# Attention products with v in two steps, some row sums over added halves, and u products over 384 columns

## The chip, the cores and the metric

The kernel runs on one NeuronCore of a Trainium2 chip. The metric is the device time of one execution in microseconds; three executions were timed, and one more was profiled.

## The reference, cut to what matters

Four batches of 576 rows go through block-causal attention (8 heads of 64), then a feed-forward layer with a convolution over neighbouring rows, then a second feed-forward layer that mixes rows.

```python
scores = scale * q @ k.T                        # per head, 576 x 576
scores = where(block_i >= block_j, scores, -1e9)  # blocks of 64 rows
attn = exp(scores - max); attn /= attn.sum(-1) + 1e-9
x = concat_heads(attn @ v)                      # 4 x 576 x 512
h = relu(x @ w_in); c = conv3(h); x = (h * sigmoid(c)) @ w_out       # 512 -> 1024 -> 512
h = relu(x @ w2_in); u, v = split(h, 2)         # 512 each
v = (v - mean(v)) / sqrt(var(v) + 1e-6)
out = (u * (w_spatial @ v + b_spatial)) @ w2_out
```

## The kernel before

The heads are taken two at a time: 16 pairs. Every value is split into a high and a low half where the products need it, so most products are three matmuls with one result (high by high, low by high, high by low).

**Steps.** Work on TensorE (PE) is cut into steps, and the string SEQ (line 64) writes out their order by hand, one letter a step. An x or y is one of the five steps of a pair's row maxima: four products of queries and keys, which VectorE (DVE) reduces, and a transposition (line 1005) after which the maxima go by DMA into a row that enters the scores. An s is a score step (lines 1062 to 1074), after which ScalarE (ACT) takes the exponential (line 1083) into the tiles e0 and e1. A v is the product of the exponentials with v (function av, line 1111; matmuls on line 669). An m is a product of the first feed-forward layer (in1, out1; matmuls on line 661), a p one of the second layer. An f is a filling step: two matmuls of 222 columns with no use for their result. A capital letter takes its PSUM buffer from the other ring. The string has 432 letters, 3 of them f.

**Forms on PE.** The x, s and v steps use the array in parts (64 rows, or 64 or 32 columns); the last of the row-maximum products, the transpositions, m and p use the whole array.

**Other engines.** ORDER (line 70) holds the order of every instruction on DVE, ACT, GpSimd (POOL) and the DMA queue of SyncE (SP); BIND says which buffer each step gets; ENG says on which engine an operation with a choice runs. All four are tables written out in the source, and an engine takes its next entry only when that entry's turn has come. Each engine therefore waits in order.

**Row sums.** For the pairs in ONES_PAIRS (0 to 5) the sums of the exponentials are made on PE, with a column of ones over all five chunks of keys (68 matmuls in the av step, sums included). For the other ten pairs add_up (line 1142) adds the chunks up in a tile es on DVE or POOL (lines 1155 and 1156, table ADD), and PE takes one short sum of it (36 matmuls in the step). The normalisation norm_a multiplies in three pieces for the first kind, in one for the second.

**Second layer.** x2 lies in DRAM. For each batch load_x2s brings it whole into one tile (one buffer), load_tails brings the last 64 rows of two batches into another. Steps: vtile (12 matmuls over 512 columns), ustep (12 matmuls over 288 columns; 8 a batch, 32 in all), sstep (mixing over rows, then the product with u on DVE), ostep (the last product). The raw weights of the last stage go through two buffers of the ring wr.

## Time and profile before

| | us |
|---|---|
| median of 3 runs | 578.49 (577.84 to 578.58) |
| the profiled execution's own time | 578.16 |
| its span in the trace | 576.4 |
| PE busy in it | 566.5 (98%) |
| VectorE busy | 420.9 (73%) |
| ScalarE busy | 259.7 (45%) |
| GpSimd busy | 121.7 (21%) |

The span runs from the first to the last instruction of the trace. Rows of the trace have a start and a duration; a matmul's duration holds its way through the array, so the rate at which PE works is read from start to start. A stretch is counted from the span's start.

### The profile page before, as it was taken

How to read it: one execution, taken by the hardware profiler on the slowest of the kernel's cores; microseconds unless marked ns; L12 is line 12 of the kernel's file. 1: busy time of each engine (PE TensorE's matmuls, PEld its weight loads, DVE VectorE, ACT ScalarE, POOL GpSimd, SP SyncE). 2: the span in 40 equal slices, each digit the busy share in tenths (PEclk: the TensorE clock that was granted, in tenths of full speed). 3: DMA queues.
4: the chain of work that ended last, by engine and by line, in shares of the span. 5: the costliest groups of instructions: out<-in, count | busy, mean ns of one | idle time of the engine just before them, and what ended most of it. 6: DMA issues, size and time to landing. Idle time of an engine off the chain costs nothing.

```text
span 576.4 us, 11721 instructions
## 1 busy us (share of the span) xinstructions
PE 566.5 (98%) x4570; PEld 510.2 (89%) x4570; DVE 420.9 (73%) x954; ACT 259.7 (45%) x554; POOL 121.7 (21%) x166
## 2 busy tenths in 40 slices
PE   7999999999999999999999999999999999999997
PEld 5666689798988888899889999999899989999997
DVE  5888889977498889869574788566996446456557
ACT  6657668643576336437262766443351014014101
POOL 4334312130013312401311020333111111012020
PEclk7999999999999999999999999999999999999999
DMA  7677642031404143130214547138203230330002
GB/s 229 208 216 202 223 155 75 30 108 45 125 25 148 46 127 127 28 121 2 65 43 152 190 144 215 43 115 251 97 1 124 72 91 1 124 102 22 33 31 84
DMA packets 43430, 61.13 MB, mean 106 GB/s; under 512 B 8877, under 2 KB 34221, under 8 KB 43374
## 3 DMA queue, kind: packets, MB, share of 16 engines
q1 hardware_dynamic: 43230, 60.37, 33.7%
q8 instruction: 36, 0.59, 0.4%
q14 instruction: 20, 0.16, 0.1%
q10 hardware_dynamic: 144, 0.00, 0.0%
HBM read 45.99 MB, written 14.23 MB: 104 GB/s over the span
## 4 chain that ended last, share of the span: by engine, by line
PE 95%; DVE 2%; ACT 1%; POOL 1%; issue 0%; DVEq 0%; POOLq 0%; ACTq 0%
PE mo L661 57%; PE s L661 14%; PE st L669 10%; PE st L1070 4%; PE st L1062 4%; PE st L943 2%; PE st L1074 2%; PE st L661 1%; DVE mx L948 1%; PE mo L1384 1%; ACT e L1083 1%; DVE y L1669 0%; PE st L1005 0%; POOL x L698 0%; POOL w1i_l L698 0%
## 5 line engine op out<-in xcount | busy, mean ns | idle before, releaser
L661 PE MATMUL mo<-x,w1i_h 128*128 128x290 f32 x504 | 105.7, 299 | 0.0
L661 PE MATMUL mo<-g,w1o_h 128*128 128x288 f32 x464 | 97.7, 297 | 0.0
L661 PEld LDWEIGHTS mo<-x,w1i_h 128*128 128x128 f32 x504 | 82.4, 188 | 2.1 <-ACT g L691 0.5
L661 PEld LDWEIGHTS mo<-g,w1o_h 128*128 128x128 f32 x464 | 76.0, 189 | 2.0 <-issue 1.6
L1241 DVE SCALAR_TENSOR_TENSOR cc<-h,cwt,cc 128x288 f32<-128x288 f32 x128 | 66.3, 532 | 12.0 <-ACT cc L1238 11.1
L661 PE MATMUL mo<-x,w1i_l 128*128 128x290 f32 x252 | 74.8, 297 | 0.0
L661 PE MATMUL mo<-g,w1o_l 128*128 128x288 f32 x232 | 68.5, 295 | 0.0
L1083 ACT ACTIVATE e<-st 128x1024 f32<-128x1024 f32 (+2 forms) x64 | 53.2, 837 | 21.1 <-PE st L1074 20.4
L661 PE MATMUL mo<-x,w2i_h 128*128 128x288 f32 x256 | 51.8, 295 | 0.0
L948 DVE TENSOR_REDUCE mx<-st 128x2 f32<-128x128 f32 (+2 forms) x64 | 42.4, 684 | 8.6 <-PE st L943 8.3
L661 PEld LDWEIGHTS mo<-x,w1i_l 128*128 128x128 f32 x252 | 47.5, 188 | 0.0
L669 PE MATMUL st<-e,v 128*64 128x448 f32 (+4 forms) x384 | 46.7, 392 | 0.1
L669 PEld LDWEIGHTS st<-e,v 128*64 128x64 f32 x384 | 25.0, 137 | 22.9 <-issue 16.8
L661 PEld LDWEIGHTS mo<-g,w1o_l 128*128 128x128 f32 x232 | 43.6, 188 | 0.0
L672 POOL TENSOR_SCALAR g<-ga 128x288 fp32r<-128x288 f32 x40 | 20.1, 513 | 110.8 <-DVE ga L1589 44.0
L661 PEld LDWEIGHTS mo<-x,w2i_h 128*128 128x128 f32 x256 | 41.2, 188 | 0.4 <-ACT u L1563 0.2
L698 POOL TENSOR_TENSOR g<-cc,g 128x288 fp32r<-128x288 f32 x19 | 18.1, 954 | 106.4 <-ACT g L691 74.0
L661 PE MATMUL s<-w2i_h,x 128*128 128x512 f32 x128 | 39.5, 390 | 0.0
L661 PE MATMUL mo<-ws_h,vnh 128*128 128x288 f32 x135 | 39.4, 296 | 0.0
L661 PE MATMUL mo<-x,w2i_l 128*128 128x288 f32 x128 | 37.7, 295 | 0.0
L1074 PE MATMUL st<-mq,mk 64*128 64x320 f32 (+1 forms) x192 | 37.2, 383 | 0.0
L1238 ACT ACTIVATE cc<-h,cwt 128x288 f32<-128x288 f32 x64 | 33.9, 533 | 5.6 <-DVE g L675 2.8
(200 smaller groups left out, 1327.8 us busy)
## 6 DMA issues: line engine op xcount, KB each, us to landing
x2d<-y SPq DMA_DIRECT2D x32, 288.0 KB
x<-x2d SPq DMA_DIRECT2D x16, 576.0 KB
raw<-in_kq_dram SPq DMA_DIRECT2D x15, 576.0 KB
v<-in_vt_dram SPq DMA_DIRECT2D x16, 320.0 KB
rb<-rd SPq DMA_DIRECT2D x32, 144.0 KB
x<-in_w2i_dram SPq DMA_DIRECT2D x8, 512.0 KB
out_dram<-o SPq DMA_DIRECT2D x28, 144.0 KB
w_raw<-in_w1i_dram SPq DMA_DIRECT2D x4, 512.0 KB
```

Of the source, the lines that this page charges most:

```text
L661: nc.tensor.matmul(o, w, x, start=start, stop=stop)
L669: nc.tensor.matmul(o[row:row + m], w, x, start=start, stop=stop)
L672: nc.gpsimd.tensor_scalar(o, i, 1.0, 0.0, ALU.mult, ALU.add)
L698: P=("POOL", t_ptt(n), lambda: nc.gpsimd.tensor_tensor(o, a, b, ALU.subtract), 0, prio, True))
L943: nc.tensor.matmul(st[:, e, o:o + n], qp[r, 128 * c:128 * c + 128], kp[r, 0:n], start=True, stop=True)
L948: return ("DVE", t_dve(2 * i.shape[-1] * (i.shape[2] if len(i.shape) == 4 else 1)), lambda: nc.vector.tensor_reduce(o, i, AX.X, ALU.max), ...
L1062: nc.tensor.matmul(out, keys(RAW[p][:, 0, :], r), RAW[p][r, 1, q0:q0 + nq], start=True, stop=False)
L1070: nc.tensor.matmul(st[:, e, o:o + nq], keys(kx, slice(64 * e, 64 * e + 64)), qx[e], start=j == 0, stop=False)
L1074: nc.tensor.matmul(st[:, e, o:o + nq], keys(mk, r), q[r, q0:q0 + nq], start=False, stop=True)
L1083: yield ("ACT", t_act(2 * n), lambda: nc.scalar.activation(ex[:, :, e0:e0 + n], st[:, :, 0:n], ACTF.Exp, scale=0.125), 0, 0)
L1238: yield ("ACT", t_act(HT, False, 1), lambda: nc.scalar.activation(cc, h[:, o:o + HT], ACTF.Copy, scale=cwt[:, c, 1:2]), 0, P_G)
L1241: yield ("DVE", t_dve(HT, ptr=1), lambda: nc.vector.scalar_tensor_tensor(cc, h[:, o + e:o + e + HT], cwt[:, c, j:j + 1], cc, ALU.mult, ALU ...
```

## The change

Four things are edited, and every table is written anew. (1) ONES_PAIRS loses pairs 3 to 5: their sums now go by add_up, and their av steps have the shorter form. (2) Each av step becomes two steps, one for the key chunks 0, 1 and 4 and one for the chunks 2 and 3 with the sums; the first doesn't need the last exponential, and SEQ has 32 v for 16. (3) ustep takes 384 columns of a pair of batches: three column pieces a pair of batches, 24 steps for 32; x2 comes in tiles of 384 columns with two buffers, the middle one from both batches; the tile of tails is gone, a tile ux holds 192 columns of u, and the product with u on DVE takes two pieces where it crosses the tiles. (4) The ring wr of the last stage has one buffer for two. SEQ, ORDER, BIND and ENG are all new; SEQ has 450 letters, 13 of them f.

```diff
-ONES_PAIRS = 0x3f
+ONES_PAIRS = 0x7
...
 SEQ = (
-    "xxxyxyxsssfsxxssfxyxxvxssssxyxxvxssssxyxxvxssssxyxxvxssssxyxxvsxsfxssyxxvxsmmmmmxxmmxxxmmmmsssmmssvxmxxxmmssxm"
-    "mmmxMmmmxmmmxxvxsmmmxsssssmmmmmmmxmxxvxssmmmmmxvssssssmmmmxxvxssxmmmmxxmxxvssmmxssmxmxmmxxvsxmsssxmxmxxvsmmxsm"
-    "mssmmmxmmmmmmmmmMmmmmmmsvsssmmmmmvmmmmmmmmmmmmmmmmmmmmMmmmmmmmmmmmppmmmmMmmmpppppppppppppppppppppppppppppppppp"
-    "pPppPpPpPPpPppppppPpppppppppppppppppppPPPPPPppPPPppppPppppppppppppppppppPPPPPPppPppppppppPpppPpPpPpPpp"
+    "xxxysxyxsfssxffffxssffxyxxvvfxsfsssxyxxvvxssssxyxxvvxssssxyxxvvsxsssxfyxxvfsfxfsvxyssxxmmmmmvvxsmmxxmxxxmmssss"
+    "svvxmxmxxxmmmssmmmmmMmxmxmmxxvvsmmmmxsmmmxssssmmmxmvvxxmmxssmmxmssvvmmssssmmmmmxxvvxssxmmmmxxxxmmmsvvsssxmmmxx"
+    "xxmvxsvsssmmmmxxmmxxvvxsmmsmmssxmmmmmvvsmmmMmmmmmmsssmmmmmvvmmmmmmmmmmmmmmmmmmmmMmmmmmmmmmmmpppmmmmMmmmppppppp"
+    "pppppppppppppppppppppppPppPpPpPPpPppppppPpppppppppppppppppppPPPPPPppPPPppppPppppppppppppppPPPPPPppPppppppppPpp"
+    "pPpPpPpPpp"
 )
...
-    "K": "AAPPDPAAADDADAADP",
+    "K": "DPAPPAPPDADPDPADD",
-    "ADD": "PPPPPPPPDDDDPPPPDDDDDDDDDDDDDDPDDDDDDDPDDDDDDDPPDDDDDDDPDDDPDDDD",
+    "ADD": "PPPPPPPPDDDDDDDDDPPDDPDDDDDDDDDPPDDDDDDDPDDPDPPPDDDDPPDPDDDDDDDD",
...
-        self.cost = 0.1 if tile != self.tile else 0.0
+        self.cost = 0.15 if tile != self.tile else 0.0
...
-    def av(p):
+    def av(p, part):
+        chunks = ((0, 1, 4), (2, 3))[part]
+
         def fn(got):
-            st = got["st"][0]
-            AVT[p] = st.rearrange("p b n -> p (b n)")
-            a, v = AVT[p], VT[p]
+            if part == 0:
+                AVT[p] = got["st"][0]
+            st = AVT[p]
+            a, v = st.rearrange("p b n -> p (b n)"), VT[p]
             ex = [ES[p, g] for g in range(2)]
             ops = []
-            for c, (k0, q0, et, e0) in enumerate(CH):
+            for c in chunks:
+                k0, q0, et, e0 = CH[c]
                 for lo, hi in ((0, 128), (128, S)) if c == 0 else ((q0, S),):
                     ops += [(a[:, VO + lo:VO + hi], 64 * e, v[:, e, c, :], ex[et][:, e, e0 + lo - q0:e0 + hi - q0],
-                             c == 0, hi == 128 or c == 4) for e in range(2)]
-            if pe_sums(p):
+                             c == 0, hi == 128 or c == 3) for e in range(2)]
+            if part == 1 and pe_sums(p):
                 for c, (k0, q0, et, e0) in enumerate(CH):
                     for lo, hi, o, j in QSEG:
                         lo = max(lo, q0)
                         if lo < hi:
                             ops += [(a[:, lo - o:hi - o], 64 * e + 32 * j, ones4 if c == 4 else ones,
                                      ex[et][:, e, e0 + lo - q0:e0 + hi - q0], c == 0 and lo > 0, c == 4 - j) for e in range(2)]
-            else:
+            elif part == 1:
                 es = SUMS[p]
+                od.cost += 0.18
                 for src, lo, hi, j in ((ex[0], 0, 128, 0), (es, 128, HT, 0), (es, HT, S, 1)):
                     o = 0 if src is ex[0] else 128
                     ops += [(a[:, lo - HT * j:hi - HT * j], 64 * e + 32 * j, ones, src[:, e, lo - o:hi - o], True, True)
                             for e in range(2)]
             tiled(ops)
-            od.cost += 0.18
+            if part == 0:
+                return None
+            AVT[p] = a
             return [(v_out(p, st), "att"), (s_out(p, st), "att"), (st_out(p, st), "att")]
-        return dict(needs=[("e", p, g, i) for g in range(2) for i in range(2)] + [("v", p)] + ([] if pe_sums(p) else [("sum", p)]),
-                    rings=[("st", 1)], fn=fn,
+        if part == 0:
+            return dict(needs=[("e", p, 0, 0), ("e", p, 0, 1), ("e", p, 1, 0), ("v", p)], rings=[("st", 1)], fn=fn, tile=True)
+        return dict(needs=[("e", p, 1, 1)] + ([] if pe_sums(p) else [("sum", p)]), rings=[], fn=fn,
                     frees=lambda: [("v", [VT[p]]), ("e0", [ES[p, 0]]), ("e1", [ES[p, 1]])] + ([] if pe_sums(p) else [("es", [SUMS[p]])]), tile=True)
 
     def add_up(p):
@@ -1296,7 +1306,7 @@
         if p == 0:
             sstream.extend(score(p, 0, i, part) for part in range(2) for i in range(2))
         sstream.extend(score(p, g, i) for g in range(p == 0, 2) for i in range(2))
-        vstream.append(av(p))
+        vstream.extend(av(p, part) for part in range(2))
...
-    X2, XT = {}, {}
+    X2 = {}
+    NT = 384
+    PIECES = [[(0, 0, NT, 0)], [(0, NT, S, 0), (1, 512, S, 192), (1, 0, 128, 256)], [(1, 128, 512, 0)]]
+    U_OUT = [[(0, 0, NT, 0)], [(0, NT, S, 0), (2, 0, 192, 192)], [(1, 128, 512, 0)]]
+    S_IN = [[[(0, 0, HT)], [(0, HT, S)]], [[(2, 64, 192), (1, 128, HT)], [(1, HT, 512), (2, 0, 64)]]]
 
     def load_x2s():
-        for b in range(B):
-            yield ("take", "x20")
-            t = X2[b] = p2w.tile([128, 2, KD, S], F32R, name="x2", tag="x2", bufs=1)
-            for hf in range(2):
-                for m in range(KD):
-                    yield ("wait", ("x2", b, hf, m))
-                od.spawn(load_x2(b, hf, t), "p2")
-
-    def load_x2(b, hf, t):
+        for pr in range(B // 2):
+            for j, pieces in enumerate(PIECES):
+                yield ("take", "x20")
+                t = X2[pr, j] = p2w.tile([128, 2, KD, 384], F32R, name="x2", tag="x2", bufs=2)
+                for e, lo, hi, _ in pieces:
+                    for hf in range(lo >= HT, 1 + (hi > HT)):
+                        for m in range(KD):
+                            yield ("wait", ("x2", 2 * pr + e, hf, m))
+                od.spawn(load_x2(pr, j, t), "p2")
+
+    def load_x2(pr, j, t):
         def ld():
-            for i in range(2):
-                nc.sync.dma_start(out=raw(t[:, i, :, HT * hf:HT * hf + HT]), in_=x2d[b][i, :, :, HT * hf:HT * hf + HT])
-        yield from dma(od, 2 * 589824, ld, 0, 1.35)
-        yield ("mark", ("x2l", b, hf))
-
-    def load_tails():
-        for b in range(0, B, 2):
-            yield ("take", "xt")
-            t = p2w.tile([128, 2, KD, 128], F32R, name="xt", tag="xt", bufs=1)
-            XT[b] = t
-            for e in range(2):
-                for m in range(KD):
-                    yield ("wait", ("x2", b + e, 1, m))
-
-                def ld(b=b, e=e, t=t):
-                    for i in range(2):
-                        nc.sync.dma_start(out=raw(t[:, i, :, 64 * e:64 * e + 64]), in_=x2d[b + e][i, :, :, 512:S])
-                yield from dma(od, 2 * 262144, ld, 0 if b == 0 else 2, 1.35)
-            yield ("mark", ("xt", b))
+            for e, lo, hi, at in PIECES[j]:
+                for i in range(2):
+                    nc.sync.dma_start(out=raw(t[:, i, :, at:at + hi - lo]), in_=x2d[2 * pr + e][i, :, :, lo:hi])
+        yield from dma(od, 2 * 786432, ld, 0, 1.35 if len(PIECES[j]) == 1 else 3.2)
+        yield ("mark", ("x2l", pr, j))
...
+        at, o = ((b // 2, 0 if c < 3 else 1), (0, 128, 256, 0, 128)[c]) if b % 2 == 0 else ((b // 2, 2 if c else 1), (256, 0, 128, 256)[c])
...
-    def ustep(b, hf, m):
+        return dict(needs=[("w2i", 1, k) for k in range(KD)] + [("x2l",) + at], rings=[("st", 1)], fn=fn,
+                    frees=lambda: [("x20", [None])] if b % 2 and c == 0 else [])
+
+    def ustep(pr, j, m):
         def fn(got):
-            x2 = X2[b]
+            x2 = X2[pr, j]
             ring = me["ring"]
             slot = got[ring][0]
             ps = bank(slot)
             i = 0
             for k in range(KD):
                 for w, xi in ((w2i_h, 0), (w2i_l, 0), (w2i_h, 1)):
-                    mm(ps[:, 0:HT], w[:, k, 128 * m:128 * m + 128], x2[:, xi, k, HT * hf:HT * hf + HT],
-                       i == 0, i == 3 * KD - 1)
+                    mm(ps[:, 0:NT], w[:, k, 128 * m:128 * m + 128], x2[:, xi, k, :], i == 0, i == 3 * KD - 1)
                     i += 1
-            if hf == 0 and m == 0:
-                U[b] = p2w.tile([128, KD, S], F32, name="u", tag="u", bufs=1)
-            u = U[b]
+            if m == 0:
+                if j == 1:
+                    U[pr, 2] = P2[0].tile([128, KD, 192], F32, name="ux", tag="ux", bufs=1)
+                else:
+                    U[pr, j // 2] = p2w.tile([128, KD, S], F32, name="u", tag="u", bufs=1)
 
             def task():
-                yield ("ACT", t_act(HT), lambda: nc.scalar.activation(
-                    u[:, m, HT * hf:HT * hf + HT], ps[:, 0:HT], ACTF.Relu), 0, 0)
+                for e, lo, hi, at in U_OUT[j]:
+                    yield ("ACT", t_act(hi - lo), lambda: nc.scalar.activation(
+                        U[pr, e][:, m, lo:hi], ps[:, at:at + hi - lo], ACTF.Relu), 0, 0)
                 yield ("free", ring, slot)
-                yield ("mark", ("u", b, hf, m))
+                yield ("mark", ("u", pr, j, m))
             return [(task(), "p2")]
-        me = dict(needs=[("w2i", 0, k) for k in range(KD)] + [("x2l", b, hf)],
-                    base=[("u", 1)] if hf == 0 and m == 0 else [], fn=fn,
-                    frees=lambda: [("x20", [None])] if (hf, m) == (1, 3) else [])
+        me = dict(needs=[("w2i", 0, k) for k in range(KD)] + [("x2l", pr, j)],
+                    base=[("ux" if j == 1 else "u", 1)] if m == 0 else [], fn=fn,
+                    frees=lambda: [("x20", [None])] if j != 1 and m == 3 else [])
...
-                yield ("DVE", t_dve(HT), lambda: nc.vector.tensor_tensor(
-                    ga, u[:, d, HT * hf:HT * hf + HT], ps[:, 0:HT], ALU.mult), 0, 0)
+                at = 0
+                for e, lo, hi in S_IN[b % 2][hf]:
+                    x, y = slice(at, at + hi - lo), U[b // 2, e][:, d, lo:hi]
+                    yield ("DVE", t_dve(hi - lo), lambda: nc.vector.tensor_tensor(ga[:, x], y, ps[:, x], ALU.mult), 0, 0)
+                    at += hi - lo
...
-        pstream.extend(ustep(b, hf, m) for hf, m in tiles)
+        pstream.extend(ustep(b // 2, j, m) for j in ((2,) if b % 2 else (0, 1)) for m in range(KD))
...
-    od.spawn(load_tails(), "p2")
...
-    slots("wr", p2, 2, [128, 1152], F32, "w_raw")
+    slots("wr", p2, 1, [128, 1024], F32, "w_raw")
```

## Rows read from the trace of the kernel before

**Rows 1.** Page, part 1: busy us (share of the span) xinstructions of each engine.
```profile
PE 566.5 (98%) x4570; PEld 510.2 (89%) x4570; DVE 420.9 (73%) x954; ACT 259.7 (45%) x554; POOL 121.7 (21%) x166
```

**Rows 2.** Page, part 4: chain that ended last, share of the span by engine and line.
```profile
PE 95%; DVE 2%; ACT 1%; POOL 1%; issue 0%; DVEq 0%; POOLq 0%; ACTq 0%
```

**Rows 3.** Stretches: us, busy us (x instructions) by engine, PEclk, DMA share, GB/s.
```profile
10.00:20.00 10.00, 10.00 (x69) 6.97 (x70) 8.05 (x20) 7.82 (x17) 2.53 (x3) 0.76 0.73 236
17.25:67.25 50.00, 48.30 (x575) 33.39 (x571) 41.19 (x100) 31.42 (x49) 17.62 (x18) 1.00 0.66 199
67.25:105.60 38.35, 38.05 (x335) 31.95 (x336) 35.45 (x81) 28.79 (x61) 7.81 (x9) 1.00 0.39 127
304.00:572.00 268.00, 268.00 (x1860) 258.95 (x1861) 176.61 (x409) 87.47 (x207) 48.13 (x75) 1.00 0.32 99
```

**Rows 4.** Waits of PE: engine line waited for: us in total, times, longest us.
```profile
PE st L1005 <- DVE mx L996: 2.7, 2, 2.5
...
PE st L1070 <- ACT e L1083: 0.6, 1, 0.6
```

**Rows 5.** PE in order of time (start us, us): products with v, pairs 2 and 7.
```profile
39.23 2.92 PE L669 MATMUL st<-e,v 128*64 128x128 f32 x24
42.09 1.61 PE L669 MATMUL st<-e,ones 128*32 128x128 f32 x44
43.63 0.50 PE L943 MATMUL st<-kp,qp 64*128 64x512 f32 x2
...
134.21 2.92 PE L669 MATMUL st<-e,v 128*64 128x128 f32 x24
...
137.69 0.49 PE L943 MATMUL st<-kp,qp 64*128 64x512 f32 x2
```

**Rows 6.** Chain in order of time (start us, us, what): steps of 288 and 512 columns.
```profile
336.08 1.59 PE s L661 x12
...
409.40 10.89 PE s L661 x48
```

**Rows 7.** PE in order of time: into 64-row products, and out of them.
```profile
232.22 0.29 PE L661 MATMUL mo<-g,w1o_h 128*128 128x288 f32 x1
232.44 0.39 PE L1070 MATMUL st<-qp,kp 64*128 64x256 f32 x2
...
247.93 0.28 PE L1070 MATMUL st<-raw,kp 64*128 64x256 f32 x2
248.05 0.28 PE L1074 MATMUL st<-mq,mk 64*128 64x256 f32 x2
248.26 0.40 PE L661 MATMUL mo<-g,w1o_h 128*128 128x288 f32 x1
```

**Rows 8.** PE in order of time, first 18 us; full is the tile of the filling products.
```profile
9.56 0.38 PE L1005 MATMUL st<-ident,mx 128*9 128x128 f32 x1 [2.51 <-DVE mx L996]
...
17.28 0.40 PE L661 MATMUL mo<-full 64*128 64x222 f32 x2
17.61 0.28 PE L1005 MATMUL st<-ident,mx 128*9 128x128 f32 x1
```

**Rows 9.** DVE by line and shape, 17 to 107 us: count, busy us, mean ns.
```profile
L820 DVE SCALAR_TENSOR_TENSOR w_f<-w_raw,top 128x512 uint32<-128x512 uint32 x7 | 5.0, 709 | 0.0
...
L1155 DVE TENSOR_TENSOR es<-e,e 128x896 f32<-128x896 f32 x1 | 1.1, 1111 | 0.0
...
L1155 DVE TENSOR_TENSOR es<-es,e 128x640 f32<-128x640 f32 x1 | 0.8, 827 | 0.2 <-ACT e L1083 0.2
...
L1155 DVE TENSOR_TENSOR es<-es,e 128x384 f32<-128x384 f32 x1 | 0.6, 559 | 0.0
...
L1155 DVE TENSOR_TENSOR es<-es,e 64x128 f32<-64x128 f32 x1 | 0.3, 291 | 0.0
```

**Rows 10.** POOL and DVE in order of time around 78 us.
```profile
78.29 1.28 POOL L698 TENSOR_TENSOR w1o_l<-w_f,w1o_h 128x512 fp32r<-128x512 f32 x1 [4.28 <-ACT w1o_h L691]
...
78.37 1.38 DVE L1203 TENSOR_TENSOR xp<-xp,rb 128x160 f32<-128x160 f32 x1 [1.56 <-DMA rb<-rd]
```

More of the change, by code (lines that the diff above doesn't have):

```diff
@@ L233 @@
     "x1": (
[2 rows of a table removed]
[2 rows of a table added]
         "norm_a11:1 norm_a12:4 norm_a13:0 norm_a14:2 norm_a15:5 split643:3 split643.2:1 split643.3:3 split643.4:1 "
         "split643.5:3 split643.6:1 split643.7:4 split643.8:0"
+    ),
+    "e0": (
+        "s0:0 s6:1 s10:0 s14:1 s18:0 s22:1 s26:0 s30:1 s34:0 s38:1 s42:0 s46:1 s50:0 s54:1 s58:0 s62:1"
     ),
@@ L335 @@
 ENG = {
[L336 to L351 removed]
+    "WH": "PPDPPDPPAPPAAAAPADADDAAA",
+    "W": "PPPPDPDPDPDDDDDDPDDDDDDP",
+    "K": "DPAPPAPPDADPDPADD",
+    "Q": "AADAPDAAADDPDDPPA",
+    "QE": "PPADPDPDPPPADAAPPADPPDPPDDDAPAPA",
+    "KL": "PDPPPDPPDDDDPDDD",
+    "QL": "PDDDPDPDDDDDDDDP",
+    "M": "AADDAAAAAADADADD",
+    "ADD": "PPPPPPPPDDDDDDDDDPPDDPDDDDDDDDDPPDDDDDDDPDDPDPPPDDDDPPDPDDDDDDDD",
+    "V": "AAAAAAADAAADDADA",
+    "S": "AAAAAAAADDAAAAAA",
+    "XH": "AAADAAAAAAPAPADD",
+    "X": "PPDDPDDPDDPPDDPD",
+    "GH": "AAPAAPAPPPDPPDAADAPAAAAADAADPPAPDADAAAPAAPDDDPAAAAAAAADAAPAAPPAP",
+    "G": "DDDPDDDDPDPPPDDDPDDDDDDDPDDPDPDDPDDDDPDDDDDDDDDDDDDDDDPDDDDPDDDD",
+    "TOP": "AAAAADDDAAPPADAPAAAADAAA",
 }
@@ L648, in attn_moe_moe2_kernel @@
         "raw": NRAW, "mq": NQ, "kpq": NKP, "v": 2, "e0": NE[0], "e1": NE[1], "es": NES, "late": NRAW - 1, "xp": 2, "sr": 1, "rb": 1,
-        "mt": 2, "rc": 1, "x20": 1, "xt": 1, "tail": 2, "vf": 2, "u": 1, "cp": 0,
+        "mt": 2, "rc": 1, "x20": 2, "ux": 1, "tail": 2, "vf": 2, "u": 1, "cp": 0,
         **{("ga", hf, d): 1 for hf in range(2) for d in range(KD)},
@@ L817, in split64 @@
                   A=("ACT", t_act(512, False) + 0.17, lambda: nc.scalar.activation(o, x, ACTF.Copy), 0, prio, False),
-                  D=on("D", 512, lambda: nc.vector.tensor_copy(o, x), prio, fast=True),
-                  P=on("P", 512, lambda: nc.gpsimd.tensor_copy(o, x), prio))
+                  D=("DVE", t_dve(512, True) + 0.05, lambda: nc.vector.tensor_copy(o, x), 0, prio, True),
+                  P=("POOL", t_round(512) + 0.18, lambda: nc.gpsimd.tensor_copy(o, x), 0, prio, True))
         yield ("DVE", t_dve(512), lambda: nc.vector.scalar_tensor_tensor(
@@ L1541, in fn @@
             return [(task(), "p2")]
-        need = [("x2l", b, hf) for hf in range(1 if c < 2 else 2)] if c < 4 else [("xt", b)]
-        return dict(needs=[("w2i", 1, k) for k in range(KD)] + need, rings=[("st", 1)], fn=fn,
-                    frees=lambda: [("xt", [None])] if c == 4 else [])
-    def ustep(b, hf, m):
+        return dict(needs=[("w2i", 1, k) for k in range(KD)] + [("x2l",) + at], rings=[("st", 1)], fn=fn,
+                    frees=lambda: [("x20", [None])] if b % 2 and c == 0 else [])
+    def ustep(pr, j, m):
         def fn(got):
-            x2 = X2[b]
+            x2 = X2[pr, j]
             ring = me["ring"]
@@ L1593, in task @@
                     yield ("free", "u")
+                    if b % 2:
+                        yield ("free", "ux")
                 if hf == 0:
@@ L1613, in fn @@
             return [(task(), "p2")]
-        me = dict(needs=[("vn", b, c) for c in range(5)] + [("ws", c) for c in range(5)] + [("u", b, hf, d)],
+        me = dict(needs=[("vn", b, c) for c in range(5)] + [("ws", c) for c in range(5)] + [("u", b // 2, j, d) for j in ((0,), (0, 1), (1, 2), (1, 2))[2 * (b % 2) + hf]],
                     base=[], fn=fn, frees=lambda: [("tail", [None])] if (hf, d) == (1, 3) else [])
```

56 lines of the change are left out of this document (19 added, 37 removed), and 274 rows, old and new, of tables (BIND, ORDER).

## The prediction

> **What bounds the kernel now.** I read the engines' busy times first: PE is busy for 566.5 of 576.4 us, no other engine for more than 73% [rows 1]. The chain that ended last says the same: 95% of the span is PE [rows 2]. Then stretches, because a mean hides stages. From 304 to 572 us PE is busy for all of 268.00 us at full clock, and from 67.25 to 105.60 us for 38.05 of 38.35; only the attention stage, 17.25 to 67.25 us, leaves it 1.70 us idle [rows 3]. The waits of PE come last: the longest is 2.5 us on the first row maxima [rows 4, 8]. So after some 18 us almost every microsecond of PE work is a microsecond of the kernel, and a change is priced by counting matmuls. Ahead of that the chain of maxima on DVE sets the time: the second transposition, at 17.61 us, comes right behind a filling step that covers the wait for it [rows 8]. One caution: from 67.25 to 105.60 us DVE is busy for 35.45 of 38.35 us [rows 3]. PE is the bound there, but only just.
>
> The sum stands on the profiled execution, 578.16 us, which is 0.33 under the median of 578.49.
>
> **Part 1, the sums of pairs 3 to 5.** An av step with its sums on PE takes from 39.23 to 43.63, 4.40 us; one with added halves takes from 134.21 to 137.69, 3.48 us [rows 5]. I count 68 and 36 matmuls for the two kinds, in all 16 steps alike. Three pairs change kind: 3 x 0.92 = 2.76 us less. What comes in its place is four additions a pair, 1.11 + 0.83 + 0.56 + 0.29 = 2.79 us on DVE [rows 9]. The new table leaves all four of pair 3, the first and last of pair 4, and all but the second of pair 5 on DVE: 2.79 + 1.40 + 1.96 = 6.15 us, and three on POOL. The cover is DVE's idle time, 8.8 us between 17.25 and 67.25 and 2.9 after that [rows 3]. Where it is not there, the av step's second half waits, and everything behind it on PE. The same additions run for pairs 6 to 15 today, and PE never waits for them [rows 4]. Ends: nothing, or most of what the cover lacks; I take 0.4 us and make the far end a rival.
>
> **Part 2, u over 384 columns.** No matmul of 384 columns of this kind is in the trace, so I bound it by its neighbours. Twelve over 288 columns take 1.59 us, 132.5 ns each; 48 over 512 take 10.89 us, 226.9 ns each [rows 6]. The straight line through them gives 172.9 ns for 384, so a step of 2.075 us. Before: 32 x 1.59 = 50.9 us. After: 24 x 2.075 = 49.8 us. That is 1.1 us less; the columns are the same, only 96 fixed shares go. One end is nothing gained (cost in proportion to columns), the other 1.6 us (half as much again). PE has no idle time in that stage [rows 3], so all of it counts.
> The Trainium skill ("TensorE: Matmul & The Clock Gate", section "Back-to-back issue gap") gives a spacing of N/2.4 ns plus 2.5 ns. By that fixed share the change would save only 96 x 2.5 ns, an estimate of 0.24 us. The measured rate at 288 columns is 132.5 ns, not the 122.5 of that rule, so here the fixed share is larger and the measurement decides.
> In the same stage x2 now comes in pieces with two buffers, and a piece is asked for when its predecessor's last step ends. Between the end of the first piece and the first use of the third lie four u steps and eight mixing steps, over 20 us at these rates. With one wr buffer the weights come one behind the other, and the third piece is queued on SP behind the second of them. I price both at nothing: cover of that size; without it PE would wait at the first steps that need w2o or the third piece. ACT and DVE get a few more, shorter, operations; DVE is busy for 176.61 of 268 us there [rows 3], so these are free.
>
> **Part 3, av in two steps and the new order.** Changing between whole-array and part-array products costs PE time. Into the parts the start-to-start time is 0.22 us (232.22 to 232.44) where 0.13 is usual [rows 6, 7]; out of them 0.21 (248.05 to 248.26) where the two starts before lie 0.12 apart [rows 7]. So 0.09 us a change. Counting the letters of SEQ gives 56 changes before and 64 after; up to the second transposition, where DVE's chain sets the time, 4 and 6. So six more count: 0.55 us. Cutting av itself adds no matmul; the halves follow each other in 14 pairs, and in two other work lies between: I add 0.2 us (two more entries and exits), ends 0 and 0.4.
> The Trainium skill ("TensorEngine Tiling (Array Packing)", section "Key Properties") says that changing the mode drains the engine: it speaks against more pieces, and the 0.09 us is what it costs here.
>
> **Part 4, filling steps.** Thirteen for three. A step is two matmuls of 222 columns, by the same straight line 105 ns each, 0.21 us; the one at 17.28 takes 0.33 until the next start, with the change of form [rows 8]. Ahead of the second transposition there are 7 for 2, in DVE's shadow. Behind it, 6 for 1: 1.05 us more PE work, all before the seventh transposition. There PE idles for 1.70 us today [rows 3], and four of the six stand next to the steps that wait. So half is covered: 0.55 us (ends 0 and 1.65).
>
> **Part 5, the start.** Between the operations that end the first and the second pair's maxima DVE's list has 15 entries for 13: one 0.7 us weight operation more [rows 9] and one small one. Against it, a score step and fills stand in PE's 2.5 us gap [rows 8], after which the granted clock fell: the stretch 10 to 20 us has 0.76 [rows 3]. Should the clock hold, steps there go up to twice as fast; should it not, four fills in a row stand ahead of the last maximum product. The chain on DVE gains or loses some tenths: +0.3 us, ends -0.5 and +1.5.
>
> **Sum.** -2.76 + 0.4 - 1.1 + 0.55 + 0.2 + 0.55 + 0.3 = -1.86. The tail behind the last matmul keeps its order of work. From 578.16 this gives 576.3; I say 576.4, a tenth towards the median.
>
> **Rivals.**
> (a) The waits go too. The first half of av needs no last exponential and so can fill today's idle 1.70 us, the fills cost nothing, the clock holds at the start. Then +0.4, +0.55 and +0.3 go and another 0.9 comes back: 573.2 to 575, say 574.2. For it: the waits on ACT's exponentials are just where the fills now stand [rows 4]. Against it: PE's order stays fixed, and half of these waits are on maxima.
> (b) DVE becomes the bound before the ninth transposition. Up to it SEQ has three m steps fewer (4.8 us) and 2.76 us less av, so PE's time from 17.25 to 105.60 us, 88.35, falls to some 81.8 with fills. DVE's list up to there has 199 entries for 205: nine more additions, eight fewer operations of m steps, so its 76.6 us of work [rows 3] hardly falls. It must lose 6.5 of its 11.7 idle microseconds. It decides from where DVE cannot shed them, for it waits in order for reductions and loads. If half fails to go, PE waits 3.2 us that nothing gives back: 579.6; if all, 583. Its mechanism shows already: at 78.37 us a multiplication of 160 columns took 1.38 us while POOL ran a 1.28 us subtraction beside it [rows 10], where an addition of 384 columns takes 0.56 [rows 9]; and three additions now go to POOL.
> The Trainium skill ("SBUF — State Buffer", section "Who interferes with whom") says that a DVE operation with two SBUF inputs and a POOL operation that reads SBUF exclude each other; the trace agrees, with those 1.38 us.
> (c) The start is late. The clock stays down and the four fills delay the maxima: +1.5 instead of +0.3, 577.6.
>
> **How the numbers follow.** Forecast 0.50 (575.3 to 577.6, mostly below 577.3), (a) 0.16, (b) 0.21, (c) 0.13. The time is the forecast's, 576.4. The range 573.8 to 580.0 takes in (a) but for its low end, (c), and (b) up to half its price. About 0.2% (1.16 us) is what a measurement can tell from no change: faster means under 577.33, slower over 579.65. Faster: 0.42 + 0.16 + 0.04 = 0.62. Slower: the upper part of (b), 0.14. Same: the rest, 0.24.
>
> **What would show it.** Right: av steps of pairs 3 to 5 at some 3.5 us, u steps at 2.07, PE without waits from 67 us to the tail, the second transposition within half a microsecond of 17.6. Wrong: waits of PE on es or on maxima between 48 and 105 us, a u step of 2.12 us or more, waits on x2 or w2o behind 340 us, a second transposition after 18.5.

## The result: 581.61 us, slower

The changed kernel takes 581.61 us in the median of 4 runs (581.35 to 582.03), the kernel before, on the same chip, 578.54 (577.84 to 579.34). The ratio is 1.0053, with a 95% interval from 1.0041 to 1.0065. The forecast was 576.4, with a range to 580.0. One thing is needed to read the runs below: with some orders of the start, executions of one and the same kernel lie up to 4 us apart, so medians stand with their ranges.

PE is still the bound. Stretches of the kernel after: us, busy us (x instructions) of PE, PEld, DVE, ACT, POOL, then PEclk, DMA share, GB/s. They answer [rows 3].

```profile
21.45:70.76 49.31, 47.53 (x517) 31.80 (x516) 44.14 (x101) 28.66 (x47) 23.00 (x28) 1.00 0.69 217
70.76:109.11 38.35, 37.60 (x323) 30.62 (x320) 37.02 (x81) 27.29 (x60) 9.89 (x10) 1.00 0.28 90
308.00:575.50 267.50, 267.32 (x1769) 258.20 (x1764) 179.40 (x428) 89.06 (x211) 46.79 (x72) 1.00 0.31 95
```

DVE is now busy for 37.02 of the 38.35 us behind the seventh transposition, where it was busy for 35.45. The waits of PE in the kernel after (engine line waited for: us in total, times, longest us) answer [rows 4]:

```profile
PE st L1064 <- DVE mxu L950: 2.0, 2, 1.1
...
PE st L663 <- POOL qlast L674: 0.7, 1, 0.7
PE st L945 <- DVE mxu L950: 0.4, 1, 0.4
```

The wait of 2.5 us for the first maxima has shrunk to 0.3, and others on maxima have come. What this costs shows in order of time. PE in the kernel after, first 22 us (start us, us, what, xcount, idle before and who ended it), against [rows 8]:

```profile
8.55 1.44 PE L1064 MATMUL st<-raw 64*128 64x320 f32 x4 [1.13 <-DVE mxu L950]
10.31 0.38 PE L1007 MATMUL st<-ident,mx 128*9 128x128 f32 x1 [0.33 <-DVE mx L998]
...
14.54 0.69 PE L945 MATMUL st<-kp,qp 64*128 64x384 f32 x2 [0.37 <-DVE mxu L950]
15.03 1.45 PE L663 MATMUL mo<-full 64*128 64x222 f32 x6
...
20.91 0.62 PE L663 MATMUL mo<-full 64*128 64x222 f32 x4
21.45 0.28 PE L1007 MATMUL st<-ident,mx 128*9 128x128 f32 x1
```

The second transposition comes at 21.45 us, 3.84 later than the 17.61 of [rows 8]. The six filling matmuls at 15.03 us lie about 0.21 us apart, the four at 20.91 about 0.11: PE ran at 1.2 GHz for some 5 us longer than before, up to 19.9 us. (The rows ahead of that read a granted clock of 1.00 in this trace, because it has no record of the clock's level there; the spacing of equal matmuls tells it.) The kernel before, where the level is on record, has 0.50 from 8 us on and comes up at 14.8. Its stretches, with the columns as above:

```profile
8.00:9.00 1.00, 0.00 (x0) 0.00 (x0) 1.00 (x5) 0.77 (x2) 0.85 (x2) 0.50 0.99 295
14.00:15.00 1.00, 1.00 (x7) 0.56 (x6) 0.60 (x1) 0.93 (x3) 1.00 (x2) 0.59 1.07 385
```

The other parts did what their steps say. PE in the kernel after: products with v of pair 3 and the step behind them, and six matmuls of u:

```profile
54.76 2.92 PE L671 MATMUL st<-e,v 128*64 128x128 f32 x24
...
58.33 0.81 PE L1064 MATMUL st<-raw 64*128 64x320 f32 x4
...
387.03 0.51 PE L663 MATMUL mo<-x,w2i_h 128*128 128x384 f32 x2
387.38 0.33 PE L663 MATMUL mo<-x,w2i_l 128*128 128x384 f32 x1
387.55 0.51 PE L663 MATMUL mo<-x,w2i_h 128*128 128x384 f32 x2
387.90 0.33 PE L663 MATMUL mo<-x,w2i_l 128*128 128x384 f32 x1
388.07 0.51 PE L663 MATMUL mo<-x,w2i_h 128*128 128x384 f32 x2
```

Pair 3 takes 3.57 us where [rows 5] has 4.40 for such a step. Six matmuls of u take 1.04 us. In the table, "second" to "seventh" are the starts of the transpositions, counted from the one at 9.56 us of [rows 8]; the last stage begins with its first 512-column product and ends with the start of PE's last instruction. All in us; the medians are of all runs, the rest is of the one profiled execution.

| kernel | first at | second at | second to seventh | seventh to last stage | last stage | median (range) |
|---|---|---|---|---|---|---|
| before | 9.56 | 17.61 | 49.92 | 287.50 | 217.48 | 578.54 (577.84 to 579.34) |
| after | 10.31 | 21.45 | 49.31 | 288.49 | 216.83 | 581.61 (581.35 to 582.03) |
| e1 | 10.42 | 18.36 | 49.54 | 287.57 | 216.77 | 577.72 (577.50 to 578.24) |
| e2 | 10.11 | 19.00 | 49.32 | 288.82 | 216.80 | 580.09 (579.22 to 582.09) |
| e3 | 10.27 | 19.92 | 49.55 | 287.81 | 216.85 | 579.40 (578.73 to 579.78) |
| e4 | 9.95 | 21.12 | 49.71 | 287.13 | 217.54 | 581.21 (580.49 to 581.84) |
| e5 | 10.39 | 18.73 | 49.56 | 287.57 | 216.82 | 577.32 (576.99 to 577.97) |
| e6 | 10.46 | 18.25 | 48.54 | 287.54 | 216.82 | 577.02 (576.20 to 577.98) |
| e7 | 10.31 | 18.53 | 51.33 | 288.35 | 216.83 | 580.32 (580.13 to 581.46) |
| e8 | 10.29 | 18.70 | 48.47 | 287.56 | 216.95 | 576.84 (576.53 to 577.73) |
| e9 | 10.13 | 18.15 | 51.64 | 289.43 | 216.83 | 582.76 (581.33 to 584.06) |
| e13 | 10.48 | 18.87 | 52.67 | 291.80 | 216.81 | 585.59 (585.31 to 586.08) |

After against before: +3.84 up to the second transposition, -0.61, +0.99 (0.7 of it the wait for qlast above), -0.65. The start eats more than the rest gives.

### The profile page after: what moved, and what is told of

It is laid out like the page before. It is cut to its first block, busy times and chain, and to the rows that moved or that the text cites. A ratio compares the mean times of both kernels' runs of the same rounds, so it can differ in the third digit from the quotient of the medians.

```text
span 579.6 us, 11391 instructions
## 1 busy us (share of the span) xinstructions
PE 570.3 (98%) x4398; PEld 509.3 (88%) x4398; DVE 429.6 (74%) x973; ACT 254.8 (44%) x546; POOL 134.3 (23%) x177
## 4 chain that ended last, share of the span: by engine, by line
PE 94%; DVE 3%; ACT 1%; issue 1%; POOL 0%; DVEq 0%; POOLq 0%; ACTq 0%
PE mo L663 56%; PE s L663 14%; PE st L671 9%; PE st L1072 4%; PE st L1064 3%; PE st L945 2%; PE st L1076 2%; PE st L663 1%; DVE mx L950 1%; PE mo L1394 1%; DVE w1i_l L677 1%; DVE raw L677 0%; ACT e L1085 0%; POOL qlast L674 0%; PE st L1007 0%
## 5 line engine op out<-in xcount | busy, mean ns | idle before, releaser
L663 PE MATMUL mo<-x,w1i_h 128*128 128x290 f32 x504 | 106.9, 300 | 0.0
L1251 DVE SCALAR_TENSOR_TENSOR cc<-h,cwt,cc 128x288 f32<-128x288 f32 x128 | 65.3, 526 | 15.7 <-ACT cc L1248 14.8
L663 PE MATMUL mo<-x,w2i_h 128*128 128x384 f32 x192 | 49.4, 335 | 0.0
L674 POOL TENSOR_SCALAR g<-ga 128x288 fp32r<-128x288 f32 x40 | 21.3, 540 | 103.7 <-DVE ga L1594 43.4
L663 PE MATMUL s<-w2i_h,x 128*128 128x512 f32 x144 | 44.4, 389 | 0.0
L671 PEld LDWEIGHTS st<-e,v 128*64 128x64 f32 x384 | 22.5, 137 | 22.3 <-issue 16.7
L1076 PE MATMUL st<-mq,mk 64*128 64x320 f32 (+1 forms) x192 | 38.9, 389 | 0.0
L1245 ACT ACTIVATE h<-mo 128x290 f32<-128x290 f32 x63 | 25.6, 409 | 27.6 <-PE mo L663 22.7
L663 PEld LDWEIGHTS mo<-x,w2i_h 128*128 128x128 f32 x192 | 34.7, 188 | 0.2
L1253 ACT ACTIVATE cc<-cc 128x288 f32<-128x288 f32 x64 | 27.5, 439 | 14.6 <-DVE cc L1251 14.2
## 6 DMA issues: line engine op xcount, KB each, us to landing
raw<-in_kq_dram SPq DMA_DIRECT2D x15, 576.0 KB
```

The source lines that it names most:

```text
L663: nc.tensor.matmul(o, w, x, start=start, stop=stop)
L671: nc.tensor.matmul(o[row:row + m], w, x, start=start, stop=stop)
L674: nc.gpsimd.tensor_scalar(o, i, 1.0, 0.0, ALU.mult, ALU.add)
L1076: nc.tensor.matmul(st[:, e, o:o + nq], keys(mk, r), q[r, q0:q0 + nq], start=False, stop=True)
L1245: yield ("ACT", t_act(290), lambda: nc.scalar.activation(h[:, 1:291], ps[:, 0:290], ACTF.Relu), 0, 0)
L1251: yield ("DVE", t_dve(HT, ptr=1), lambda: nc.vector.scalar_tensor_tensor(cc, h[:, o + e:o + e + HT], cwt[:, c, j:j + 1], cc, ALU.mult, ALU ...
```

## The experiments

### The start: e1 to e4

e1 is the changed kernel with the old letters at the start of SEQ, e2 moves only the early score step (the fifth letter) back, e3 takes out five of the seven fills and keeps the early step, e4 is the kernel before with the new letters at its start.

```diff
-    "xxxysxyxsfssxffffxssffxyxx...    (after; e4: the kernel before with this)
+    "xxxyxyxsssfsxxssfxyxx...         (e1)
+    "xxxyxyxssfssxffffxssffxyxx...    (e2)
+    "xxxysxyxsfssxxssfxyxx...         (e3)
```

> The changed kernel with the first letters of SEQ as before: the early score step s0 back behind the second pair's first maximum products, two filling steps for seven ahead of the second transposition; all else, DVE's order too, is the changed kernel's. Theory 'PE at the start' (the second transposition comes 3.84 us late, 21.45 for 17.61 us, because PE runs at the half clock until 19.9 us and has a score step and five fills more in its way): the second transposition at 17.6 to 18.5 us and a total of 578 to 579 us. Theory 'DVE at the start' (its new order with two entries more holds the maxima back): second transposition not before 19.3, total over 580.3.

> The changed kernel with only the early score step s0 put back behind the second pair's first maximum products; the seven fills stay. Theory 'PE at the start': first transposition back from 10.31 to about 9.6 us, the second by 0.7 to 1.5, total 580 to 581 us. If the score step alone is the cause: 578 to 578.7. Theory 'DVE at the start': no change, 581.5.

> The changed kernel with five of the seven fills ahead of the second transposition taken out; s0 stays early. Theory 'PE at the start': ten matmuls at 0.21 us less, second transposition 1 to 2.1 us earlier, total 579.5 to 580.6 us. If the fills are what will bring the clock up, taking them out costs more than it gives: 582 or more. Theory 'DVE at the start': 581.5.

> The kernel before with the first letters of SEQ as in the changed one: s0 early and seven fills; all else is the kernel before. Theory 'PE at the start': second transposition at 20.5 to 21.5 us, total 581.5 to 582.5 us. Theory 'DVE at the start': 578.3 to 579.3 us, since DVE's order is the old one.

Ratios to the kernel before: e1 0.9992 (0.9983 to 1.0001), e2 1.0038 (1.0023 to 1.0054), e3 1.0015 (1.0006 to 1.0024), e4 1.0051 (1.0038 to 1.0064). The theory that DVE's order makes the start late fell in all four; the other had the second transposition right in e1, e3 and e4, while e2's came earlier than it said. The letters alone cost 2.8 us on the kernel before and give 3.9 back on the changed one: they are the whole loss, and more. Of the 3.9, 3.1 lies ahead of the second transposition and 0.9 behind the seventh, where the kernel after waits 0.7 us for GpSimd's rounding of qlast and e1 doesn't. Neither half does it alone. By the traces' records of the clock and the spacing of equal matmuls, PE's clock is up at 14.8 us in the kernel before, 14.2 in e1, 15.1 in e2, 19.1 in e3, 19.7 in e4 and 19.9 in the kernel after. Summing times from start to start by kind of step up to the second transposition, the kernel after has 8.03 us of score steps for 4.91 before (36 matmuls in both) and 2.28 of fills (14 matmuls) for 0.54 (4); the full-array maximum products, with the wait behind the first, fell from 3.79 to 2.72. In e2 1.2 us of the loss is elsewhere: PE waits that long for qlast behind 100 us, since GpSimd's rounding of it began late (its input had landed late) and took 2.29 us beside DVE's work, where e1 has 0.64.

### The later fills: e5 and e10

The six fills behind the second transposition are taken out, in e5 from e1, in e10 from e6.

```diff
-...xxvvfxsfsssxyxx...xfyxxvfsfxfsvxyss...
+...xxvvxssssxyxx...xyxxvsxsvxyss...
```

> The changed kernel with the old start letters (e1, 577.72 us) and without the six filling steps that stand behind the second transposition; the two of the old start stay. Theory, that each of them is work added to a TensorE that is always late: in e1's trace they take 0.84 us together, so about 576.9. Rival, that they stand where TensorE would wait for VectorE or ScalarE anyway: the waits come back, about 577.7, and the table of TensorE's waits has new rows between 20 and 75 us.

> e6 and e5 together: x18 ahead of the subtraction, and the six later filling steps out. Theory from e5, that the fills stand in places where TensorE would wait anyway: the time is that of e6, 577.0 within 0.3 us, and what the fills took (1.4 us) comes back as longer x, s and v steps between the second and the seventh transposition. Rival, that they are work in the path, as their cost of 0.84 us was summed for e1: 576.2.

e5: 577.32, ratio 0.9985 (0.9977 to 0.9994); e10: 577.03 (576.16 to 577.93), ratio 0.9966 (0.9953 to 0.9979), against 577.72 and 577.02 with the fills. From the second to the seventh transposition e1 has 49.54 us and e5 49.56: the fills' 1.40 us are gone, and x steps take 6.53 for 5.81, score steps 19.70 for 19.08, v steps 20.72 for 20.40. PE's waits do come back in e5 (0.6 us on ACT's exponentials for 0.3, 0.3 on maxima), as the rival has it: most of the fills' time stood where PE waits anyway. The times don't settle how much. e5's median lies halfway between theory and rival, and its trace is of its slowest execution, e1's of its fastest. e10's median is that of e6, but by the ratios, each taken against the kernel before on the same chip, e5 is 0.4 us under e1 and e10 0.7 under e6, with overlapping intervals. So the fills cost between nothing and 0.7 us. (e10's profiled execution, 577.93, was the slowest of its five and is not read for these stages.)

### One subtraction among GpSimd's instructions: e6 and e8

e6 is e1 with one change of order on DVE; e8 adds three more moves at the start.

```diff
-  ... x17 split64.7 x18*2 split64.9 x15 max_up3 ...
+  ... x17 x18*2 split64.7 split64.9 x15 max_up3 ...
 e8 also, on DVE:
-  one000 one010 x0*2 ... x3*2 ends1 max_up0 ... x8*2 split64.3 max_up1
+  one000 x0*2 ... x3*2 max_up0 ends1 ... x8*2 max_up1 split64.3    (one010 goes to POOL)
```

> e1 with one change of order on VectorE between the third and the fourth transposition: the two reductions of step x18 stand ahead of the weight subtraction of slice 7 instead of behind it. In e1 that subtraction took 3.15 us where its like take 0.68, while GpSimd ran four instructions back to back, and TensorE waited 0.9 us for the reductions behind it. Theory, that the wait is only the order on VectorE: the 0.9 us wait goes and the time is 576.8. Rival, that VectorE has no slack there and the lost 2.4 us come back at the next reduction or at the fourth maximum: 577.5 to 577.8, with a wait of like size at the fourth transposition.

> e6 with three more moves: the second half of the first keys is rounded on GpSimd instead of VectorE, the odd ends of pair 1 stand behind the first maximum on VectorE, and the split of slice 3 behind the second. In e1 the first transposition came at 10.42 us and the second at 18.36, where the kernel before had 9.56 and 17.61. Theory, that the start is bound by VectorE's order: both transpositions come 0.4 to 0.8 us earlier, and the time is 0.5 to 0.8 below e6, 576.0 to 576.3. Rival, that TensorE at half clock bounds this stretch: the second transposition moves by under 0.2 us and the time is that of e6.

DVE in e1, and POOL in e1, in order of time:

```profile
34.42 3.15 DVE L677 TENSOR_TENSOR w1i_l<-w_f,w1i_h 128x512 fp32r<-128x512 f32 x1
37.50 1.08 DVE L950 TENSOR_REDUCE mx<-st 128x2 f32<-128x896 f32 x1
```

```profile
34.28 0.24 POOL L674 TENSOR_SCALAR qlast<-raw 64x64 fp32r<-64x64 f32 x1
34.49 0.67 POOL L674 TENSOR_SCALAR kp<-raw 128x576 fp32r<-128x576 f32 x1
35.13 1.27 POOL L700 TENSOR_TENSOR w1i_l<-w_f,w1i_h 128x512 fp32r<-128x512 f32 x1
36.37 0.67 POOL L674 TENSOR_SCALAR qp<-raw 128x576 fp32r<-128x576 f32 x1
```

A subtraction that takes 0.68 us elsewhere took 3.15, as long as POOL's train ran, and the reduction behind it came when PE had long waited. DVE and PE in e6:

```profile
34.98 1.09 DVE L950 TENSOR_REDUCE mx<-st 128x2 f32<-128x896 f32 x1 [0.50 <-PE st L945]
35.99 0.28 DVE L950 TENSOR_REDUCE mxu<-st 128x2 f32<-128x128 f32 x1
36.18 1.35 DVE L677 TENSOR_TENSOR w1i_l<-w_f,w1i_h 128x512 fp32r<-128x512 f32 x1
```

```profile
37.72 0.79 PE L1064 MATMUL st<-raw 64*128 64x320 f32 x4
```

The same step starts at 37.72 without a wait (38.83 behind a wait of 0.90 in e1), the stretch to the seventh transposition is 1.00 shorter, and the time 577.02, ratio 0.9978 (0.9970 to 0.9987): the theory held, 0.7 us in the medians. e8 has 576.84, ratio 0.9977 (0.9968 to 0.9985); its second transposition came at 18.70, 0.45 later than e6's, where the clock was up 2.6 us earlier (13.6 for 16.2); e5 and e10, with the clock up at 16.3 and 16.0, have 18.73 and 18.68. Its rival held in the time, and the three moves bring nothing at the start. The intervals of e5, e6, e8 and e10 lie below both kernels.

### The sums and the split: e7, e9 and e13

e7 is e1 with ONES_PAIRS at 0x3f again and without the additions of pairs 3 to 5. e9 is e6 with the products with v in one step, at the place of the second. e13 is e9 with the change of e7.

```diff
-ONES_PAIRS = 0x7         (e7, e13; their add_up3 to add_up5 out of all tables)
+ONES_PAIRS = 0x3f
-        vstream.extend(av(p, part) for part in range(2))      (e9, e13)
+        vstream.append(av(p))
```

> e1 with one part undone: the sums of pairs 3 to 5 are taken by TensorE over the keys again, and VectorE and GpSimd make no added halves for them (their normalisation falls into three multiplications again, as before). The products with v stay in two steps. Theory, that the part is worth what the steps' lengths say: 3.50 us for a step where it was 4.39, 2.3 to 2.7 us in three pairs, so 580.0 to 580.4. Rival, that VectorE's work for the adds (2.8 us a pair) has delayed the maxima and eaten part of it: 1.0 to 1.9 us, so 578.7 to 579.6.

> e6 with one part undone: the products with v of a pair are one step again, at the place of the second of the two steps (in 14 of 16 pairs the two stand side by side; in pairs 4 and 12 seven and two letters lie between). Theory, that the split is worth next to nothing: the changes of form that it adds for pairs 4 and 12 go, the time is that of e6 (577.02) within 0.3 us. Rival, that the split of pair 4 hides a wait, since its first step runs while the last scores of the pair are turned into exponentials: the time rises by 0.5 to 1.0 us, 577.5 to 578.0, with a new wait of TensorE between the fifth and the sixth transposition.

> e9 (the products with v in one step, 582.76 us) with the sums of pairs 3 to 5 taken by TensorE again as in e7. It tells what the waits of e9 come from. Theory, that VectorE is behind between the fifth and the sixth transposition because of the added halves, and that the first step of v covers this: without the halves the 1.8 us wait of e9 there goes, and the time is that of e7 less what x18 first is worth, 579.4 to 580.2, plus the 1.7 us of waits at pair 12 that has no part in the sums: 581 to 582. Rival, that the order of the other work alone makes the waits: they stay, and the sums' 2.6 us are added to e9: 585.0 to 585.6.

e7: 580.32, ratio 1.0041 (1.0028 to 1.0055). The sums are worth 2.6 us, as the theory had it. Of this 1.79 lies before the seventh transposition (pairs 3 and 4) and 0.78 behind it (pair 5).

e9: 582.76, ratio 1.0068 (1.0054 to 1.0082), 5.7 us over e6 by the medians and 4.9 by the profiled executions. The theory fell, and the rival was right in kind but far too small. PE in e9, then the stretches of e9, then PE in e6 at the same place:

```profile
60.36 0.44 PE L944 MATMUL st<-kp,qp 64*128 64x384 f32 x2 [0.34 <-ACT e L1084]
62.63 0.37 PE L662 MATMUL mo<-full 64*128 64x222 f32 x1 [1.82 <-DVE mxl L984]
```

```profile
60.00:62.00 2.00, 0.46 (x4) 0.19 (x2) 2.00 (x4) 0.94 (x2) 1.22 (x1) 1.00 0.01 2
62.00:64.00 2.00, 1.37 (x12) 1.38 (x13) 2.00 (x7) 0.00 (x0) 1.75 (x2) 0.76 0.80 267
64.00:66.00 2.00, 2.00 (x16) 1.88 (x14) 1.94 (x4) 1.81 (x3) 0.67 (x1) 0.50 0.64 180
```

```profile
60.23 0.45 PE L945 MATMUL st<-kp,qp 64*128 64x384 f32 x2 [0.34 <-ACT e L1085]
60.61 2.06 PE L671 MATMUL st<-e,v 128*64 128x128 f32 x16
62.59 0.37 PE L663 MATMUL mo<-full 64*128 64x222 f32 x1
```

DVE does the same work in both between 60 and 63 us. In e6 the first step of v, 2.06 us, stands in that wait. In e9 PE has nothing, and the clock falls to 1.2 GHz behind the wait (0.50 in the row 64 to 66 us): 10.97 us between the sixth and the seventh transposition (the expectation counted one less) for 8.09. At pair 12, where the steps are apart too, PE waits 0.97 and 0.66 us on DVE in e9, and that pair's stretch is 1.82 us longer.

e13: 585.59, ratio 1.0128 (1.0115 to 1.0142). The rival held: the sums' 2.8 us come on top. The waits of PE in e13:

```profile
PE mo L662 <- DVE mxl L984: 1.4, 1, 1.4
...
PE st L944 <- DVE mxu L949: 1.0, 1, 1.0
PE st L1071 <- DVE mxu L949: 0.7, 1, 0.7
```

Without the additions the wait of 1.8 us is still 1.4: most of it is the way of maxima through DVE, not the additions. So the split covers a wait that this order has anyway. The order was written for the split: the kernel before, with one step, has no wait on DVE's mxl in its list, and these runs don't tell what a split would be worth there.

### What makes the clock late: e11, e12 and e14 to e16

All five are e6 but for these letters at the start.

```diff
     "xxxyxyxsssfsxxssfxyxx...     (e6)
+    "xxxysxyxsfssfxxssfxyxx...    (e11)
+    "xxxysfxyxsfssfxxssfxyxx...   (e12)
+    "xxxyxsyxsfssxxssfxyxx...     (e14)
+    "xxxyxyxssfssxxssfxyxx...     (e15)
+    "xxxysxyxssfsxxssfxyxx...     (e16)
```

> e6 with the early score step of e3 (the letters of the start as in e3) and one more filling step, right before the x step that waited 0.37 us for VectorE at 14.50 us in e3. Theory, that this short break of TensorE keeps the clock at 1.2 GHz: in e3 the stretch from 10.27 us on is unbroken but for it, and in e1 the clock is up 3.8 us after the start of such a stretch (10.42 to 14.2). With the break covered the clock is up at 14 to 15 us, the second transposition comes at 18.2 to 18.8 us, where e3 had 19.92, and the time is that of e6, 576.8 to 577.4. Rival, that the clock stays down for the early step itself: up at 19 us or later, second transposition at 19.9 to 20.4, and 1.5 to 2 us above e6, 578.5 to 579.0.

> e11 with one more filling step, ahead of the first transposition, where TensorE waited 0.60 us in e3 (10.27 us). Theory, that TensorE's breaks keep the clock down: as e11 or earlier, the clock up by 14 us and the second transposition at 18.0 to 18.6 us, 576.6 to 577.2; and if one break alone is not the cause, this kernel has the gain and e11 has not. Rival, the early step itself: clock up at 19 us or later, 578.5 to 579.2.

> e6 with the early score step behind the first transposition instead of ahead of it; the letters behind it as in e3. TensorE then has no work in the gap ahead of the first transposition, as in e6, and the order behind it is that of e3 but for this step. Theory, that the short burst of work in the gap is what makes the clock come up late: up at 13.5 to 16.3 us as in the nine traces without it, second transposition by 18.9 us, 576.7 to 577.5. Rival, that the order behind the transposition does it: up at 17 us or later, second transposition behind 19.3 us, 578.0 to 579.0.

> e6 with one letter moved: the first filling step of the start stands behind the second score step of pair 0 instead of behind the third, where e2, e3, e11, e12 and e14 had it too. No score step is moved. Theory, that the place of the early score step makes the clock late: nothing changes here, 576.6 to 577.4 with a spread under 2 us. Rival, that the place of this filling step does it: some executions 2 us longer, a spread over 2.5 us and a median of 578 or more.

> e6 with the early score step ahead of the first transposition, as in e3, but the first filling step behind the third score step, as in e6. Theory, that the early step makes the clock late: up at 17 us or later in the profile, second transposition behind 19.3 us, a median of 578.0 to 579.0. Rival, the place of the filling step: a median of 576.6 to 577.4 and a spread under 2 us.

| kernel | median (range) | ratio to before | profiled execution | second transposition, clock up |
|---|---|---|---|---|
| e6 | 577.02 (576.20 to 577.98) | 0.9978 (0.9970 to 0.9987) | 576.43 | 18.25, 13.6 |
| e11 | 578.51 (576.93 to 579.94) | 0.9998 (0.9988 to 1.0007) | 579.94 | 20.71, 20.0 |
| e12 | 577.98 (577.06 to 581.16) | 1.0001 (0.9988 to 1.0014) | 577.89 | 19.31, 17.4 |
| e14 | 579.59 (577.19 to 580.24) | 1.0017 (1.0003 to 1.0031) | 577.36 | 19.17, 15.6 |
| e15 | 578.30 (576.35 to 580.15) | 0.9999 (0.9986 to 1.0011) | 580.14 | 20.72, 19.9 |
| e16 | 578.74 (577.46 to 580.33) | 1.0004 (0.9994 to 1.0014) | 579.19 | 19.25, 17.5 |

Covering the breaks (e11, e12) leaves the clock late: that theory fell. Without work in the gap (e14) the profiled execution is early, but six of nine are 2 us longer: neither side held. Moving no score step at all, only one fill by one letter (e15), gives a range of 3.8 us, as its rival said; the early score step with the fill at its old place (e16) gives the late clock and the median of its theory. So either move alone is enough, and no single one is the cause. PE in e15:

```profile
10.53 0.39 PE L1007 MATMUL st<-ident,mx 128*9 128x128 f32 x1 [2.80 <-DVE mx L998]
...
16.18 1.76 PE L1064 MATMUL st<-raw 64*128 64x448 f32 x4
...
18.60 1.40 PE L1064 MATMUL st<-raw 64*128 64x320 f32 x4
```

and the same two steps in e6:

```profile
15.31 1.02 PE L1064 MATMUL st<-raw 64*128 64x448 f32 x4
...
16.62 0.78 PE L1064 MATMUL st<-raw 64*128 64x320 f32 x4
```

In e15 PE shows no wait behind the one at 10.53 us up to 20 us and yet runs at half rate up to 19.9. What is shown: with the old letters the clock was up between 13.6 and 16.5 us in all eight traces of the changed kernel that have them, and no such kernel with v in two steps had a range of over 1.8 us. e1, e5, e6, e7 and e10 have the same order of work up to there, and their clocks came up at 13.6 to 16.3 us (e5, e6 and e7, on one chip, at 16.3, 13.6 and 16.0), so the moment differs between executions of one and the same start. Every other order of the start that was tried has slower executions. Which property of the order decides stays open.

These ranges are not the clock's alone. From the second to the seventh transposition e15 takes 49.77 us for e6's 48.54, at full clock, and 1.10 of that lies between the fourth and the fifth. DVE and POOL there in e15, then PE, then DVE in e6:

```profile
41.77 1.35 DVE L1213 TENSOR_TENSOR xp<-xp,rb 128x160 f32<-128x160 f32 x1 [0.33 <-DMA rb<-rd]
41.53 1.41 POOL L700 TENSOR_TENSOR raw<-raw,kp 128x576 fp32r<-128x576 f32 x1 [1.50 <-PE st L1076]
43.58 0.45 PE L945 MATMUL st<-kp,qp 64*128 64x384 f32 x2 [1.04 <-DVE mt L1013]
```

```profile
38.43 0.32 DVE L1213 TENSOR_TENSOR xp<-xp,rb 128x160 f32<-128x160 f32 x1
```

In e15 a weight tile landed late (ACT waited 0.98 us for it), DVE behind it was late, and its multiplication came beside a subtraction of POOL that it precedes in e6. The same wait of PE, 0.9 to 1.2 us, is in the profiled executions of e10, e15 and e16, and not in those of e6, e8, e11, e12 and e14. It is a second source of spread that has no part in the start.

The Trainium skill ("TensorE: Matmul & The Clock Gate", section "Part 1: The HAM clock gate") says that the moment of the rise is not tied to the kernel and varies from run to run. The five traces of one start agree; the half microsecond that it gives for this does not, with 13.6 to 16.3 us among them.

## Why the prediction was wrong

**Part 5, the start, is the step that failed.** It stood at +0.3, with +1.5 as its far end; it was +3.8 at the second transposition, and the old letters give 3.9 back (e1). Rival (c) named what happened (the clock stays down, the fills delay the maxima) and priced it with that same +1.5. The error was to price the clock by the moved work alone. While the clock is down every step goes at half rate, and it came up 5.1 us later: score steps up to the second transposition went from 4.91 to 8.03 us, fills from 0.54 to 2.28 with ten matmuls more, and only the full-array maximum products, with their wait, got shorter, from 3.79 to 2.72. I also took it that a step in PE's gap might hold the clock. It started at 8.55 us, behind a wait of 1.13 for a buffer that DVE's first reductions free, and in the kernel before the granted clock is at 0.50 from 8 us on; I looked at neither. Why the clock comes up so late with the new letters stays open.

**Part 1 was right.** The v steps lost 2.30 us by their times from start to start (2.76 forecast, less 0.2 for the cut), and e7 gives 2.6 with what hangs on them. PE never waited for es.

**Part 2 was right for u, and the stage kept 0.65 of it.** 384 matmuls over 288 columns took 51.15 us from start to start (132.5 ns each, but for two at 389 us that took 0.53 together), 288 over 384 columns 50.02 (173.7 each): 1.12 us less, or 0.86 without those two, where 1.1 was forecast. The last stage became only 0.65 shorter, since the last product (w2o) took 45.42 us for 44.97; 0.34 of this is one matmul at 567.48 us, behind which PE waits for DVE's o; this speaks against DVE's added operations being free there. Nothing waited for x2 or the weights.
The fixed share of the Trainium skill ("TensorE: Matmul & The Clock Gate", section "Back-to-back issue gap"), from which an estimate of 0.24 us came, does not fit this row either: 160 + 2.5 ns for 384 columns by the rule, 173.7 measured. The section gives the rule for a matmul by itself; here each has a weight load of its own (4398 of either in the kernel after).

**Part 3 stands as far as it was measured.** Against the kernel before, e7, which has its sums, takes 0.85 us more between the seventh transposition and the last stage, where all six added changes of form lie and 0.55 was forecast; between the second and the seventh it takes 1.41 more, of which 0.9 is the wait behind one subtraction (e6). The changes of form were not measured by themselves. What the part lacked is that the new order needs the split: where other work lies between its two steps (pairs 4 and 12), the first half stands in a wait on DVE, and without it this order is 4.9 to 5.7 us slower (e9). Rival (a) had the mechanism in words, a first half that fills idle time, and a price of 0.9. Against the kernel before, whose order has no such wait, none of this is shown to be a gain.

**Part 4 was not settled.** 0.55 was forecast; e5 and e10 leave between nothing and 0.7. The waits that come back in e5 speak for rival (a), the fills replace waits, at least in part.

**Rival (b) came in small.** DVE did not bound the whole stretch; 44.14 of 49.31 us is much, though, and one subtraction beside POOL's train cost PE 0.9 us (e6 gave 0.7 back). Its mechanism, the 1.38 us of [rows 10], was read rightly. Its price of 3.2 us was not reached; e9 shows one reason, for without the split PE waits on DVE for 1.82 us at pair 4 and 1.63 at pair 12.
The Trainium skill ("SBUF — State Buffer", section "Who interferes with whom") has this exclusion; the trace agrees, with 3.15 us for 0.68.

Without Part 5 the sum would have said 576.0; e1 has 577.7. The rest is, by its largest pieces, 0.9 of that subtraction, 0.4 in the last product, and a second transposition 0.75 later than before also with the old letters; the tail behind PE's last start, 0.38 shorter, goes the other way. From the second transposition on e6 takes 552.9 us where the kernel before takes 554.9.
